# Causal score products in halves, new planner constants, and unread products early on TensorE

## The chip, the cores and the metric

The kernel runs as one program on one core of one Trainium2 chip. The metric is the device time of one execution in microseconds. Engines are named as in the profile: PE is TensorE's products, PEld its weight loads, DVE is VectorE, ACT is ScalarE, POOL is GpSimd, and SP issues the transfers from and to memory.

## The reference

A gated linear attention runs over 768 steps for 4 batches of 8 heads with 48 columns each; its output is the input of a layer of 8 experts, of which each token takes at most one. Cut to what matters:

```
a_re, a_im: scaled to a magnitude of at most 0.999
for t in range(S):                       # S = 768, per batch and head
    S_re, S_im = (a_re*S_re - a_im*S_im) + k[t] v[t]^T,  a_re*S_im + a_im*S_re
    y[t] = q[t] @ S_re
x = y as (3072 tokens, 384)
e = argmax(x @ w_gate); g = softmax(x @ w_gate)[e]; run only if x @ w_skip > 0
out = x + g * (relu(x @ w1[e]) @ w2[e])  # else out = x
```

## The kernel before

The recurrence is done in chunks of 128 steps: 6 chunks by 4 batches make 24 units, numbered u. For each unit the complex gate is turned into angles and decays ("gates": logarithms, exponentials and sines on ACT, sums over the steps as the triangular products `pt` and `pl` on PE). q and k are scaled and turned (`qe`, `w`, on DVE), transposed on PE (`tp`), and copied from PSUM (`wT`, on ACT). Inside a chunk the score of a key step and a query step matters only where the query is not earlier than the key. `pa` is the score product, four heads at a time: for each head a 96 by 128 weight (the keys) and 128 moving columns (the queries), all 128 by 128 scores, and `at` on DVE multiplies them by a triangular mask that zeroes the early queries. `py` makes the unit's output from the masked scores and the values `vt`, and from the state `Sb` that the chunks before have left. Its outputs are 64 wide, so that an even head writes PSUM partitions 0 to 63 and the odd head beside it 64 to 127. `ps` adds to the state, `yT` and `px` give the tokens and the routing scores.

After the last unit come the experts, eight after another: `ph` and `po` are their two products, and the gathered tokens `xg` come from memory, two buffers deep. Splitting the experts' weights into two parts on ACT and DVE (`h` and `l` in the trace) begins in the last units.

All operations of a unit are put into a list with an engine, a duration, a due time, what they need, and what buffers they take. `Plan.order` plays this list through: of the operations that can begin about as early as any, the one with the earliest due time is next on its engine. The instructions are then written in that order, and each engine works through its own in order. `STARTS`, `LEADS`, `TRIG`, `READY`, `PULL` and the other constants at the top set the due times; they say which units' gates go together and how early loads are asked for. SP issues all loads from one queue. fp32 products stand twice in the trace: each is two records, with a weight load each.

Of the kernel before, what the change touches and what calls it, by code (L numbers as in the profile page):

```python
# [10 lines left out]
F32 = mybir.dt.float32  # L11
F32R = mybir.dt.float32r
BF16 = mybir.dt.bfloat16
I32 = mybir.dt.int32
# [15 lines left out]
NEAR, COLD = 0.1, 33.0  # L30
WAFTER, WGAP, CHECK = 0.75, 0.21, 2
ROOMS = dict(ain=6, tr=5, U=6, cs=2, e=5, qk=4, w0=2, w1=2, wT0=2, wT1=2, vt=3, at=2, st=2, yT=2, row=4, G=1, raw=2, raw2=4,
             tp=2, pa=2, y=1, g=1, c=2, xa=3, mpt=2, mph=3, mpo=3, xg=2, xh=2, hh=2, og=2)
# [14 lines left out]
class Plan:  # L48
# [3 lines left out]
    OVER = dict(P=0.0, A=0.105, V=0.085, G=0.0)  # L52

    def __init__(self, rooms):
        self.rooms, self.ops, self.rel = rooms, {}, {}

    def add(self, key, eng, us, at, need=(), take=(), free=()):
        def put(fn):
            need_ = list(need)
            if (key[0], key[1] - 1) + key[2:] in self.ops and key[0][:2] not in ("rt", "ro", "re"):  # L60
                need_.append((None, (key[0], key[1] - 1) + key[2:]))
            self.ops[key] = (eng, us, at, need_, list(take), fn)
            for x in free:
                self.rel.setdefault(x, []).append(key)
        return put

    def order(self):
        end, free, held, out = {}, dict.fromkeys("PAVGS", 0.0), {"xa": [("xa", "z")]}, []
        pipe, warm = 0.0, [-9.0, 0.0]

# [31 lines left out]
        while todo:  # L102
            can = {}
            for key in todo:
                r, e = ready(key), self.ops[key][0][0]
                if r is not None:
                    can.setdefault(e, []).append((max(r, free[e]), self.ops[key][2], key))
            assert can, sorted(todo, key=str)[:9]
# [3 lines left out]
            todo.remove(key)  # L112
            eng, us, at, need, take, fn = self.ops[key]
            if len(eng) > 1:
                free[e] = max(s, pipe - 6.0) + (0.97 if e == "G" else 0.4 * int(eng[1]))
                pipe = max(free[e] + 0.9, pipe) + us
                end[key] = (free[e], "D", pipe + 1.0)
            else:
                if e == "P":
                    if s - warm[0] > 3.0:  # L120
                        warm[1] = 0.0
                    if s < COLD or warm[1] < 4.0:
# [12 lines left out]
        assert len(out) == len(self.ops), sorted((k for k in self.ops if k not in end), key=str)[:9]  # L135
        self.end = end
# [3 lines left out]
class Kern:  # L140
# [12 lines left out]
    def consts(self, ctx):  # L153
# [12 lines left out]
        for t, x in ((self.mask, 1.0), (self.turns, 0.5 / math.pi)):  # L166
            g.memset(t, x)
            sel(t, [[1, 128]], ALU.is_ge, 0.0, 0, -1)
        self.tri = cst.tile([128, 128], BF16, name="tri")
        g.memset(self.tri, 1.0)  # L170
# [78 lines left out]
    def gates(self, u, k, t, end):  # L249
# [59 lines left out]

        @add(("pt", u), "P", 0.75, t1, [("on" if c else "atan", u)], take=[("c", "pt", u)])  # L310
# [33 lines left out]

        @add(("pl", u), "P", 0.72, t2, [("U", u), ("pt", end - 1)], take=[("c", "pl", u)], free=[("U", u)])
# [43 lines left out]
    def ready(self, u, t):  # L389
# [15 lines left out]
        for k in range(2):  # L405
# [6 lines left out]
            for hh in range(2):  # L412
                @add(("tp", u, k, hh), "P", 0.455, t, [("w", u, k)], take=[("tp", u, k, hh)], free=[(f"w{k}", u)])
                def _(k=k, hh=hh):
# [18 lines left out]
    def unit(self, u):  # L433
# [6 lines left out]

        @add(("lv", u), "S1", 1.0, t - PULL, take=[("vt", u)])
        def _():
            vt = X["vt", u] = self.vts[u % len(self.vts)]
            nc.sync.dma_start(vt[:, :, 0:D], self.rows(self.v, c, b))

        for hh in range(2):
            @add(("pa", u, hh), "P", 0.91, t, [("wT", u, k, hh) for k in range(2)], take=[("pa", u, hh)], free=[("wT1", u)])
            def _(hh=hh):
                pa = X["pa", u, hh] = self.ps_at.tile([128, 4, C], F32, name=f"pa_{nm}_{hh}", tag="pa")
                for h in range(hh * 4, hh * 4 + 4):  # L450
                    PE.matmul(pa[:, h % 4], X["wT", u, 1][:, h], X["wT", u, 0][:, h], start=True, stop=True)  # L451

            @add(("at", u, hh), "V", 0.686, t, [("pa", u, hh)], take=[("at", u)], free=[("pa", u, hh)])
            def _(hh=hh):
                if ("at", u) not in X:
                    X["at", u] = self.un.tile([128, H, C], F32, name=f"at_{nm}", tag="at", bufs=self.rooms["at"])
                V.tensor_tensor(X["at", u][:, hh * 4:hh * 4 + 4], X["pa", u, hh],  # L457
                                self.mask.rearrange("p (o t) -> p o t", o=1).to_broadcast([128, 4, C]), ALU.mult)

# [6 lines left out]
        if not late:  # L466
            @add(("ps", u), "P", 1.41, t, [("w", u, 1), ("lv", u)], take=[("g", "ps", u)], free=[("w1", u), ("vt", u)])
            def _():
                ps = X["ps", u] = self.ps_g.tile([96, H, D], F32, name=f"ps_{nm}", tag="g")
                for h in range(H):  # L470
                    PE.matmul(ps[:, h], X["w", u, 1][:, h].rearrange("p k d -> p (k d)"), X["vt", u][:, h, 0:D], start=True, stop=True)

# [8 lines left out]
        for hh in range(2):  # L481
            @add(("py", u, hh), "P", 0.97 if c else 0.48, t,
                 [("at", u, hh), ("lv", u)] + ([("Sb", u), ("wT", u, 0, hh)] if c else []),
                 take=[("y", u)], free=[("at", u), ("vt", u), ("wT0", u)] + [("st", u)] * (c > 0))
            def _(hh=hh):
                if X.get("yof") != u:
                    X["yof"] = u
                    X["py"] = self.ps_y.tile([128, H // 2, C], F32, name=f"py_{nm}", tag="py")
                vt, at, qT, py = X["vt", u], X["at", u], X["wT", u, 0], X["py"]
                for hp in range(hh * 2, hh * 2 + 2):  # L490
                    for j in range(2):
                        PE.matmul(py[j * 64:j * 64 + 64, hp], vt[:, 2 * hp + j], at[:, 2 * hp + j], start=True, stop=(c == 0))  # L492
                    if c > 0:
# [9 lines left out]

        @add(("px", u), "P", 0.9, t, [("yT", u), ("wg", 0)], take=[bank], free=[("yT", u)])
        def _():
# [188 lines left out]
    def attention(self):  # L694
        with ExitStack() as ctx:
# [4 lines left out]
            self.ff, self.st, self.un = P("ff", 3), P("st", 2), P("un", 2)  # L700
            self.ps_tp, self.ps_at = P("ps_tp", 2, space=PSUM), P("ps_at", 2, space=PSUM)
# [3 lines left out]
            self.vts = [pers.tile([128, H, 64], F32, name=f"vt{i}") for i in range(self.rooms["vt"])]  # L705
            self.sts = [pers.tile([96, H, 64], F32, name=f"st{i}") for i in range(self.rooms["st"])]
            for t in self.vts + self.sts:
# [4 lines left out]
            self.pieces()  # L712
            self.order = self.plan.order()
# [103 lines left out]
    def experts(self):  # L817
# [26 lines left out]
        for e in range(E):  # L844
            te = T0 + TE * e

            @add(("xg", e), "S1", 1.1, te - 0.9, [("px", u)] + [(f"re{b}", 8) for b in range(B)], take=[("xg", e)])
            def _(e=e):
                xg = X["xg", e] = self.xp.tile([128, 2, XW], F32, name=f"xg_{e}", tag="xg")
                nc.sync.dma_start(xg, self.xs[e * CAP:(e + 1) * CAP].rearrange("(t p) d -> p t d", p=128))  # L850

            @add(("idx", e), "G", 0.2, te - 0.8, [("xg", e)])
            def _(e=e):
                X["idx", e] = self.xp.tile([128, 2], I32, name=f"idx_{e}", tag="idx")
                G.tensor_copy(X["idx", e], X["xg", e][:, :, DM])
# [18 lines left out]
            for j in range(NF):  # L874
                @add(("ph", e, j), "P", 1.08, te + j * 0.11,
                     [(x, e, t) for x in ("xh", "xl") for t in range(2)] + [("wl", e, k) for k in range(KD)] +
# [21 lines left out]
            for t in range(2):  # L898
                for j in range(NF):
                    @add(("po", e, t, j), "P", 0.52, te + 0.95 + (t * NF + j) * 0.053,  # L900
                         [("hl", e, j), ("wl", e, KD + j // 2)] + [(None, ("po", e, t, j - 1))] * (j > 0) + [("px", u)] * (e == 0),
# [250 lines left out]
```

## Time and profile before

| | us |
|---|---|
| median of 3 runs | 425.59 (425.2 to 426.17) |
| the profiled execution | 426.13 |
| its span, first to last instruction | 424.4 |
| PE busy in the span | 388.5 (92%) |
| DVE busy | 319.3 (75%) |
| ACT busy | 283.9 (67%) |
| PE products before the first `pt` (14.86 us into the span) | none |
| first and last start of `pa` | 33.4 and 256.8 |
| first and last start of `py` | 41.1 and 260.9 |

The attention's units fill the span to about 264 us, the experts the rest to about 412 us, and the last rows of the output and the end of the program follow. Busy times are averages over these stages: what a change is worth is read from the stage that it touches.

### The profile page before, as it was taken

The numbers are of one execution on the slowest core, as the hardware profiler recorded it, in microseconds if no ns is written. First come the engines' busy times: TensorE is split into PE (matmuls) and PEld (weight loads), VectorE is DVE, ScalarE is ACT, GpSimd is POOL, SyncE is SP. The second block draws the span as 40 slices with busy tenths as digits, with TensorE's granted clock in tenths as the row PEclk, the third lists the DMA queues.
The fourth block names the chain that finished last, engine by engine and source line by source line (L and its number), as shares of the span: only waits on it lengthen the run. The fifth ranks groups of instructions, "written<-read, shape, count | busy, mean of one in ns | idle before, by whom it ended". The sixth has DMA issues, their size and how long they took to land. (4 is left out here: it accounts for less than half of the span.)

```text
span 424.4 us, 8790 instructions
## 1 busy us (share of the span) xinstructions
PE 388.5 (92%) x3236; PEld 346.3 (82%) x3236; DVE 319.3 (75%) x722; ACT 283.9 (67%) x550; POOL 56.6 (13%) x94
## 2 busy tenths in 40 slices
PE   0569999999999999999999988899999999999992
PEld 0248689769868987997878977799999999999992
DVE  4469799979999978987997998877666676656220
ACT  5798998889798879849898654554454655446020
POOL 7000000014005003001300121101011010111101
PEclk9967999999999999999999999999999999999998
DMA  9999929986983892444423765586665766662001
GB/s 158 184 148 171 161 58 177 366 150 142 158 168 81 139 194 54 97 80 112 101 48 119 206 213 195 159 294 223 206 236 179 233 177 230 227 192 80 27 1 33
DMA packets 148049, 65.55 MB, mean 154 GB/s; under 512 B 129323, under 2 KB 143407, under 8 KB 148000
## 3 DMA queue, kind: packets, MB, share of 16 engines
q1 hardware_dynamic: 145440, 60.29, 60.7%
q0 software_dynamic: 2560, 4.63, 3.0%
q8 instruction: 28, 0.46, 0.5%
q14 instruction: 21, 0.17, 0.1%
HBM read 52.33 MB, written 15.77 MB: 160 GB/s over the span
## 5 line engine op out<-in xcount | busy, mean ns | idle before, releaser
L810 ACT CAST h<-r 128x768 fp32r<-128x768 f32 (+1 forms) x56 | 50.8, 926 | 38.5 <-issue 19.8
L815 DVE TENSOR_TENSOR l<-r,h 128x768 fp32r<-128x768 f32 (+1 forms) x56 | 58.9, 1069 | 7.8 <-ACT h L810 7.2
L558 POOL DMA_INDIRECT xs<-xa,sl x24 | 28.9, 1206 | 231.3 <-ACT tr L242 85.0
L418 PE MATMUL tp<-ident,w 128*96 128x128 f32 x384 | 55.0, 284 | 3.0 <-ACT wT L427 1.2
L886 PE MATMUL ph<-xh,h 128*128 128x256 f32 x192 | 54.6, 288 | 1.1 <-DVE hl L896 0.8
L418 PEld LDWEIGHTS tp<-ident,w 128*96 128x96 f32 x384 | 43.1, 131 | 14.6 <-issue 4.4
L427 ACT COPY wT<-tp 96x512 f32<-96x512 f32 x96 | 52.1, 580 | 2.8 <-PE tp L418 2.6
L886 PE MATMUL ph<-xh,l 128*128 128x256 f32 x192 | 53.6, 283 | 0.0
L451 PE MATMUL pa<-wT,wT 96*128 96x128 f32 x384 | 52.4, 284 | 0.1
L886 PE MATMUL ph<-xl,h 128*128 128x256 f32 x192 | 51.8, 283 | 0.3 <-DVE xl L872 0.3
L892 ACT ACTIVATE hh<-ph 128x256 fp32r<-128x256 f32 x64 | 24.3, 383 | 40.1 <-PE ph L886 40.1
L451 PEld LDWEIGHTS pa<-wT,wT 96*128 96x128 f32 x384 | 47.9, 197 | 2.3 <-issue 0.7
L410 DVE TENSOR_TENSOR w<-qk,cs 128x768 f32<-128x768 f32 x48 | 45.3, 951 | 0.2
L907 PE MATMUL po<-h,hh 128*128 128x384 f32 x128 | 43.6, 340 | 0.0
L896 DVE SCALAR_TENSOR_TENSOR hl<-ph,hh 128x256 fp32r<-128x256 f32 x64 | 26.2, 419 | 22.4 <-ACT hh L892 22.4
L909 PE MATMUL po<-h,hl 128*128 128x384 f32 x128 | 43.0, 336 | 0.0
L908 PE MATMUL po<-l,hh 128*128 128x384 f32 x128 | 43.0, 336 | 0.0
L492 PE MATMUL py<-at,vt 128*64 128x128 f32 x384 | 37.8, 282 | 1.6 <-DVE at L457 1.2
L886 PEld LDWEIGHTS ph<-xh,h 128*128 128x128 f32 x192 | 36.7, 191 | 2.2 <-DVE hl L896 1.0
L457 DVE TENSOR_TENSOR at<-pa,mask 128x512 f32<-128x512 f32 x48 | 32.6, 684 | 7.8 <-PE pa L451 7.7
L886 PEld LDWEIGHTS ph<-xh,l 128*128 128x128 f32 x192 | 36.6, 191 | 0.0
L313 PE MATMUL pt<-tr,turns 128*128 128x384 f32 x48 | 22.1, 563 | 15.3 <-ACT tr L242 14.9
(158 smaller groups left out, 774.1 us busy)
## 6 DMA issues: line engine op xcount, KB each, us to landing
r<-in_moe_w_dram SPq DMA_DIRECT2D x24, 512.0 KB, 4.7
r<-in_moe_w_dram SPq DMA_DIRECT2D x32, 384.0 KB, 4.0
ain<-in_a_re_dram SPq DMA_DIRECT2D x24, 192.0 KB, 4.3
ain<-in_a_im_dram SPq DMA_DIRECT2D x24, 192.0 KB, 4.5
qk<-in_q_dram SPq DMA_DIRECT2D x24, 192.0 KB, 3.9
qk<-in_k_dram SPq DMA_DIRECT2D x24, 192.0 KB, 4.2
vt<-in_v_dram SPq DMA_DIRECT2D x24, 192.0 KB, 3.3
out_dram<-xa SPq DMA_DIRECT2D x5, 768.0 KB, 5.2
```

Of the source, the lines that this page charges most:

```text
L410: V.tensor_tensor(n, X["qk", u][:, k].unsqueeze(2).to_broadcast([128, H, 2, D]), X["cs", c][:, b], ALU.mult)
L418: nc.tensor.transpose(tp[:, h], n[:, hh * 4 + h].rearrange("p k d -> p (k d)"), self.ident)
L427: (V.tensor_copy if onV else A.copy)(X["wT", u, k][:, hh * 4:hh * 4 + 4], X["tp", u, k, hh])
L451: PE.matmul(pa[:, h % 4], X["wT", u, 1][:, h], X["wT", u, 0][:, h], start=True, stop=True)
L457: V.tensor_tensor(X["at", u][:, hh * 4:hh * 4 + 4], X["pa", u, hh], self.mask.rearrange("p (o t) -> p o t", o=1).to_broadcast([128, 4, C]) ...
L492: PE.matmul(py[j * 64:j * 64 + 64, hp], vt[:, 2 * hp + j], at[:, 2 * hp + j], start=True, stop=(c == 0))
L810: nc.scalar.copy(X["W", e, n][0][:, ks], X["raw", e, i])
L815: nc.vector.tensor_tensor(lo[:, ks], X["raw", e, i], hi[:, ks], ALU.subtract)
L886: PE.matmul(ph, w[:, k, ks(j)], x[:, k], start=(i == 0), stop=(i == len(terms) - 1))
L907: PE.matmul(po, hh[:, j, ks(t)], w2h[:, j], start=(j == 0), stop=False)
L908: PE.matmul(po, hh[:, j, ks(t)], w2l[:, j], start=False, stop=False)
L909: PE.matmul(po, hl[:, j, ks(t)], w2h[:, j], start=False, stop=(j == NF - 1))
```

## The change

- **Score products in halves.** `pa` is eight products for four heads in place of four: for each head the 64 early keys against all 128 queries, and the 64 late keys against the 64 late queries alone. The part that causality empties is no longer computed. Each product writes 64 PSUM partitions, and the two halves of PSUM partitions get the same number of columns. An odd head has its early keys in the upper half, so its scores stand with the key steps exchanged; a second mask `masks[:, 1]` and a second copy of its values, `vs`, fit them. `vs` is loaded by two more transfers of 64 rows by four heads each from the same values. Two PSUM tiles `pas` are zeroed once on DVE, so the part that is never written is zero.
- **The plan.** New durations for `pa`, `py`, `tp` and others, a shift of the due time for 36 kinds of operation, other `STARTS`, `LEADS`, `PULL`, `READY`, `TRIG`, and 0.1 us on a PE operation that changes between the halved products (`py`, `pa`) and the rest. For the first two units two of the four `wT` copies go to DVE (`SHARE`). `xg` has three buffers and is asked for 1.69 in place of 0.9 units ahead (`FETCH`); the final check's due time moves by one expert (`CHECK`).
- **Unread products.** Where the plan sees PE idle, from 9 us of its own time up to the first `py`, it writes `n` products of `turns` by itself (128 by 128, fp32) into a PSUM tile that nobody reads, as many as fit at 0.23 us each with 0.25 us left over. It then counts PE as warm.

```diff
-STARTS = [0, 3, 7, 11, 15, 18, 21]
-AHEAD, TRIG, READY, PULL = 3.0, 0.63, 1.05, 3.44
+STARTS = [0, 3, 7, 11, 14, 18, 21]
+AHEAD, TRIG, READY, PULL = 3.0, 1.48, 1.28, 2.95
+FILL = 9.0
+SHIFT = {'rt4': 1.08, 'xl': 0.32, 'py': -0.87, ...}
-LEADS = {0: 5.96, 1: 3.48, 2: 2.07, 3: 1.5, 4: 2.5, 5: 2.37, 6: 2.26, 7: 2.47}
-SHARE = lambda u: ((0, 1), (1, 1)) if u < 0 else ()
+LEADS = {0: 7.67, 1: 3.67, 2: 2.09, 3: 2.19, 4: 3.21, 5: 1.9, 6: 1.57, 7: 2.34}
+SHARE = lambda u: ((0, 1), (1, 1)) if u < 2 else ()
...
+            n = int((s - max(free["P"], FILL) - 0.25) / 0.23)
+            if e == "P" and n > 0 and ("py", 0, 0) not in end:
+                out.append((max(free["P"], FILL), ("fill", len(out)), lambda n=n: self.fill(n)))
+                warm = [s, 9.0]
...
-        @add(("lv", u), "S1", 1.0, t - PULL, take=[("vt", u)])
+        @add(("lv", u), "S3", 1.6, t - PULL, take=[("vt", u)])
...
+            for lo, hi in ((slice(0, 64), slice(64, C)), (slice(64, C), slice(0, 64))):
+                nc.sync.dma_start(vs[hi, :, 0:D], v[lo, 1::2])
...
-            @add(("pa", u, hh), "P", 0.91, t, ...
+            @add(("pa", u, hh), "P", 0.62, t, ...
-                for h in range(hh * 4, hh * 4 + 4):
-                    PE.matmul(pa[:, h % 4], X["wT", u, 1][:, h], X["wT", u, 0][:, h], start=True, stop=True)
+                late, early, low, high = slice(64, C), slice(0, 64), slice(0, 64), slice(64, C)
+                for i, p, ts in ((1, high, early), (1, low, late), (0, high, late), (3, low, late),
+                                 (2, high, late), (0, low, early), (3, high, early), (2, low, early)):
+                    h = hh * 4 + i
+                    t0 = 0 if ts == early else 64
+                    PE.matmul(pa[p, i, t0:], k[:, h, ts], q[:, h, t0:], start=True, stop=True)
...
+    def idle(self, n):
+        if "warm" not in self.x:
+            self.x["warm"] = self.ps_y.tile([128, H // 2, C], F32, name="warm", tag="py")
+        for i in range(n):
+            self.nc.tensor.matmul(self.x["warm"][:, 0], self.turns, self.turns, start=True, stop=True)
```

The new masks are built by five more small operations on POOL among the constants.

## Rows read from the trace of the kernel before

**Rows 1.** Busy us of each engine by stretch (instructions in brackets), clock, DMA.
```profile
0.00:14.80 14.80, 0.00 (x0) 0.00 (x0) 6.93 (x15) 9.67 (x16) 8.08 (x41) 1.00 1.19 166
14.80:26.90 12.10, 8.63 (x13) 2.98 (x13) 4.90 (x9) 9.94 (x20) 0.00 (x0) 0.90 1.19 155
26.90:38.70 11.80, 11.55 (x56) 10.26 (x56) 11.70 (x26) 9.69 (x21) 0.00 (x0) 0.53 1.02 168
38.70:60.00 21.30, 21.05 (x163) 16.44 (x164) 16.73 (x31) 20.84 (x41) 0.00 (x0) 1.00 0.85 141
...
100.00:140.00 40.00, 38.88 (x364) 32.82 (x362) 38.55 (x92) 34.95 (x72) 6.13 (x6) 1.00 0.77 145
...
264.00:300.00 36.00, 33.77 (x258) 32.50 (x257) 25.85 (x69) 17.89 (x34) 4.26 (x6) 1.00 0.71 231
```

**Rows 2.** The same view for the attention's full stretch.
```profile
43.00:264.00 221.00, 214.43 (x2067) 183.21 (x2067) 197.77 (x490) 181.29 (x359) 29.35 (x27) 1.00 0.64 143
```

**Rows 3.** What PE waited for: total us, times, longest.
```profile
PE pt L313 <- ACT tr L242: 14.9, 1, 14.9
PE pl L348 <- ACT e L242: 3.0, 1, 3.0
PE pt L862 <- DMA xg<-xs: 1.7, 4, 0.6
```

**Rows 4.** Timeline of PE, 14 to 39 us: start, length, records merged.
```profile
14.86 4.58 PE L313 MATMUL pt<-tr,turns 128*128 128x384 f32 x6 [14.86 <-ACT tr L242]
...
26.90 1.94 PE L418 MATMUL tp<-ident,w 128*96 128x128 f32 x8 [0.34 <-DVE w L410]
...
33.45 3.78 PE L451 MATMUL pa<-wT,wT 96*128 96x128 f32 x16
```

**Rows 5.** Timeline of PE, 100 to 140 us: a lone score block.
```profile
113.66 1.06 PE L451 MATMUL pa<-wT,wT 96*128 96x128 f32 x8
114.56 1.48 PE L471 MATMUL ps<-vt,w 128*96 128x48 f32 x16
```

**Rows 6.** Timeline of PE at 154 us: angle sums at full clock.
```profile
154.24 1.46 PE L313 MATMUL pt<-tr,turns 128*128 128x384 f32 x4
```

**Rows 7.** Timeline of PE, 248 to 257 us: score and output blocks in turn.
```profile
251.47 1.06 PE L451 MATMUL pa<-wT,wT 96*128 96x128 f32 x8
252.46 0.44 PE L492 MATMUL py<-at,vt 128*64 128x128 f32 x4
252.72 0.39 PE L495 MATMUL py<-wT,st 96*64 96x128 f32 x4
252.95 0.39 PE L492 MATMUL py<-at,vt 128*64 128x128 f32 x4
253.17 0.39 PE L495 MATMUL py<-wT,st 96*64 96x128 f32 x4
253.49 1.16 PE L451 MATMUL pa<-wT,wT 96*128 96x128 f32 x8
254.48 0.17 PE L646 MATMUL pr<-oh,tri 128*128 128x8 bf16 x1
```

**Rows 8.** Timeline of 0.06 us at the head of one output block.
```profile
158.39 0.14 PEld L492 LDWEIGHTS py<-at,vt 128*64 128x64 f32 x2 [0.24 <-DVE at L457]
...
158.40 0.33 PE L492 MATMUL py<-at,vt 128*64 128x128 f32 x2
```

**Rows 9.** Instructions of the output tile: ns min/median/max, first and last start.
```profile
L492 PEld LDWEIGHTS py<-at,vt x384: 132/136/138, 41.1 to 260.6; 128*64 128x64 f32 x192
```

**Rows 10.** Groups by line: busy us, mean ns of one.
```profile
L427 ACT COPY wT<-tp 96x512 f32<-96x512 f32 x96 | 52.1, 580 | 2.8 <-PE tp L418 2.6
```

**Rows 11.** Timeline of SP and of ACT near the start.
```profile
11.87 1.00 SPq L444 DMA_DIRECT2D vt<-in_v_dram  x1
...
6.26 0.61 ACT L242 ACTIVATE tr<-ain,col 128x384 f32<-128x384 f32 x1 [1.33 <-POOL twice L159]
```

More of the change, by code (lines that the diff above doesn't have):

```diff
@@ L52 @@
     OVER = dict(P=0.0, A=0.105, V=0.085, G=0.0)
+    HALVES = ("py", "pa")
     def __init__(self, rooms):
@@ L61, in put @@
                 need_.append((None, (key[0], key[1] - 1) + key[2:]))
-            self.ops[key] = (eng, us, at, need_, list(take), fn)
+            self.ops[key] = (eng, us, at + SHIFT.get(key[0], 0.0), need_, list(take), fn)
             for x in free:
@@ L68, in order @@
         end, free, held, out = {}, dict.fromkeys("PAVGS", 0.0), {"xa": [("xa", "z")]}, []
-        pipe, warm = 0.0, [-9.0, 0.0]
+        pipe, warm, mode = 0.0, [-9.0, 0.0], False
         left, users, base, todo = {}, {}, {}, set()
@@ L106, in order @@
                 if r is not None:
-                    can.setdefault(e, []).append((max(r, free[e]), self.ops[key][2], key))
+                    can.setdefault(e, []).append((max(r, free[e]) + 0.1 * (e == "P" and mode != (key[0] in self.HALVES)), self.ops[key][2], key))
             assert can, sorted(todo, key=str)[:9]
@@ L119, in order @@
                 if e == "P":
+                    mode = key[0] in self.HALVES
                     if s - warm[0] > 3.0:
                         warm[1] = 0.0
-                    if s < COLD or warm[1] < 4.0:
+                    if s < FILL + 6.0 or warm[1] < 4.0:
                         us *= 2
@@ L134, in order @@
                     start(x)
-        assert len(out) == len(self.ops), sorted((k for k in self.ops if k not in end), key=str)[:9]
+        assert len(end) == len(self.ops), sorted((k for k in self.ops if k not in end), key=str)[:9]
         self.end = end
@@ L168, in consts @@
             sel(t, [[1, 128]], ALU.is_ge, 0.0, 0, -1)
+        self.masks = cst.tile([128, 2, 128], F32, name="masks")
+        g.tensor_copy(self.masks[:, 0], self.mask)
+        m = self.masks[:, 1]
+        g.memset(m[0:64, 0:64], 0.0)
+        g.memset(m[64:128, 64:128], 1.0)
+        g.tensor_copy(m[0:64, 64:128], self.mask[0:64, 0:64])
+        g.tensor_copy(m[64:128, 0:64], self.mask[64:128, 64:128])
         self.tri = cst.tile([128, 128], BF16, name="tri")
@@ L308, in _ @@
                 V.scalar_tensor_tensor(first, X["row", u - B], -2 * math.pi, first, ALU.mult, ALU.add)
-        @add(("pt", u), "P", 0.75, t1, [("on" if c else "atan", u)], take=[("c", "pt", u)])
+        @add(("pt", u), "P", 0.73, t1, [("on" if c else "atan", u)], take=[("c", "pt", u)])
         def _():
@@ L343, in _ @@
             self.table(X["cs", c][:, b, :, 0], X["tr", u][:, 0], AF.Sin, scale=-2 * math.pi, bias=self.hpi)
-        @add(("pl", u), "P", 0.72, t2, [("U", u), ("pt", end - 1)], take=[("c", "pl", u)], free=[("U", u)])
+        @add(("pl", u), "P", 0.73, t2, [("U", u), ("pt", end - 1)], take=[("c", "pl", u)], free=[("U", u)])
         def _():
@@ L412, in ready @@
             for hh in range(2):
-                @add(("tp", u, k, hh), "P", 0.455, t, [("w", u, k)], take=[("tp", u, k, hh)], free=[(f"w{k}", u)])
+                @add(("tp", u, k, hh), "P", 0.468, t, [("w", u, k)], take=[("tp", u, k, hh)], free=[(f"w{k}", u)])
                 def _(k=k, hh=hh):
@@ L439, in unit @@
         t = float(u)
-        @add(("lv", u), "S1", 1.0, t - PULL, take=[("vt", u)])
+        @add(("lv", u), "S3", 1.6, t - PULL, take=[("vt", u)])
         def _():
-            vt = X["vt", u] = self.vts[u % len(self.vts)]
-            nc.sync.dma_start(vt[:, :, 0:D], self.rows(self.v, c, b))
+            vt, vs = X["vt", u] = self.vts[u % len(self.vts)]
+            v = self.rows(self.v, c, b)
+            nc.sync.dma_start(vt[:, :, 0:D], v)
+            for lo, hi in ((slice(0, 64), slice(64, C)), (slice(64, C), slice(0, 64))):
+                nc.sync.dma_start(vs[hi, :, 0:D], v[lo, 1::2])
         for hh in range(2):
-            @add(("pa", u, hh), "P", 0.91, t, [("wT", u, k, hh) for k in range(2)], take=[("pa", u, hh)], free=[("wT1", u)])
+            @add(("pa", u, hh), "P", 0.62, t, [("wT", u, k, hh) for k in range(2)], take=[("pa", u, hh)], free=[("wT1", u)])
             def _(hh=hh):
-                pa = X["pa", u, hh] = self.ps_at.tile([128, 4, C], F32, name=f"pa_{nm}_{hh}", tag="pa")
-                for h in range(hh * 4, hh * 4 + 4):
-                    PE.matmul(pa[:, h % 4], X["wT", u, 1][:, h], X["wT", u, 0][:, h], start=True, stop=True)
+                pa = X["pa", u, hh] = self.pas[hh]
+                q, k = X["wT", u, 0], X["wT", u, 1]
+                late, early, low, high = slice(64, C), slice(0, 64), slice(0, 64), slice(64, C)
[4 more added lines that the diff above has]
+                    PE.matmul(pa[p, i, t0:], k[:, h, ts], q[:, h, t0:], start=True, stop=True)
             @add(("at", u, hh), "V", 0.686, t, [("pa", u, hh)], take=[("at", u)], free=[("pa", u, hh)])
@@ L456, in _ @@
                     X["at", u] = self.un.tile([128, H, C], F32, name=f"at_{nm}", tag="at", bufs=self.rooms["at"])
-                V.tensor_tensor(X["at", u][:, hh * 4:hh * 4 + 4], X["pa", u, hh],
-                                self.mask.rearrange("p (o t) -> p o t", o=1).to_broadcast([128, 4, C]), ALU.mult)
+                two = lambda x: x.rearrange("p (a j) t -> p a j t", j=2)
+                V.tensor_tensor(two(X["at", u][:, hh * 4:hh * 4 + 4]), two(X["pa", u, hh]),
+                                self.masks.unsqueeze(1).to_broadcast([128, 2, 2, C]), ALU.mult)
         if c > 0:
@@ L470, in _ @@
                 for h in range(H):
-                    PE.matmul(ps[:, h], X["w", u, 1][:, h].rearrange("p k d -> p (k d)"), X["vt", u][:, h, 0:D], start=True, stop=True)
+                    PE.matmul(ps[:, h], X["w", u, 1][:, h].rearrange("p k d -> p (k d)"), X["vt", u][0][:, h, 0:D], start=True, stop=True)
             @add(("T", u), "V", 0.55, t, [("ps", u)] + [("Sb", u)] * (c > 0), free=[("g", "ps", u)] + [("st", u)] * (c > 0))
@@ L481, in unit @@
         for hh in range(2):
-            @add(("py", u, hh), "P", 0.97 if c else 0.48, t,
+            @add(("py", u, hh), "P", 0.90 if c else 0.45, t,
                  [("at", u, hh), ("lv", u)] + ([("Sb", u), ("wT", u, 0, hh)] if c else []),
@@ L488, in _ @@
                     X["py"] = self.ps_y.tile([128, H // 2, C], F32, name=f"py_{nm}", tag="py")
-                vt, at, qT, py = X["vt", u], X["at", u], X["wT", u, 0], X["py"]
+                (vt, vs), at, qT, py = X["vt", u], X["at", u], X["wT", u, 0], X["py"]
                 for hp in range(hh * 2, hh * 2 + 2):
                     for j in range(2):
-                        PE.matmul(py[j * 64:j * 64 + 64, hp], vt[:, 2 * hp + j], at[:, 2 * hp + j], start=True, stop=(c == 0))
+                        PE.matmul(py[j * 64:j * 64 + 64, hp], vs[:, hp] if j else vt[:, 2 * hp], at[:, 2 * hp + j], start=True, stop=(c == 0))
                     if c > 0:
@@ L502, in unit @@
         bank = ("c" if late else "g", "px", u)
-        @add(("px", u), "P", 0.9, t, [("yT", u), ("wg", 0)], take=[bank], free=[("yT", u)])
+        @add(("px", u), "P", 0.925, t, [("yT", u), ("wg", 0)], take=[bank], free=[("yT", u)])
         def _():
@@ L704, in attention @@
             self.rooms = dict(ROOMS)
-            self.vts = [pers.tile([128, H, 64], F32, name=f"vt{i}") for i in range(self.rooms["vt"])]
+            self.vts = [[pers.tile([128, n, 64], F32, name=f"{a}{i}") for a, n in (("vt", H), ("vs", H // 2))] for i in range(self.rooms["vt"])]
+            self.pas = [self.ps_at.tile([128, 4, C], F32, name=f"pa{i}") for i in range(2)]
+            for x in self.pas:
+                nc.vector.memset(x, 0.0)
             self.sts = [pers.tile([96, H, 64], F32, name=f"st{i}") for i in range(self.rooms["st"])]
-            for t in self.vts + self.sts:
+            for t in [x for p in self.vts for x in p] + self.sts:
                 nc.gpsimd.memset(t[:, :, D:64], 0.0)
@@ L712, in attention @@
             self.pieces()
+            self.plan.fill = self.idle
             self.order = self.plan.order()
@@ L845, in experts @@
             te = T0 + TE * e
-            @add(("xg", e), "S1", 1.1, te - 0.9, [("px", u)] + [(f"re{b}", 8) for b in range(B)], take=[("xg", e)])
+            @add(("xg", e), "S1", 1.1, te - FETCH, [("px", u)] + [(f"re{b}", 8) for b in range(B)], take=[("xg", e)])
             def _(e=e):
-                xg = X["xg", e] = self.xp.tile([128, 2, XW], F32, name=f"xg_{e}", tag="xg")
+                xg = X["xg", e] = self.xp.tile([128, 2, XW], F32, name=f"xg_{e}", tag="xg", bufs=3)
                 nc.sync.dma_start(xg, self.xs[e * CAP:(e + 1) * CAP].rearrange("(t p) d -> p t d", p=128))
@@ L874, in experts @@
             for j in range(NF):
-                @add(("ph", e, j), "P", 1.08, te + j * 0.11,
+                @add(("ph", e, j), "P", 1.1, te + j * 0.11,
                      [(x, e, t) for x in ("xh", "xl") for t in range(2)] + [("wl", e, k) for k in range(KD)] +
@@ L899, in experts @@
                 for j in range(NF):
-                    @add(("po", e, t, j), "P", 0.52, te + 0.95 + (t * NF + j) * 0.053,
+                    @add(("po", e, t, j), "P", 0.526, te + 0.95 + (t * NF + j) * 0.053,
                          [("hl", e, j), ("wl", e, KD + j // 2)] + [(None, ("po", e, t, j - 1))] * (j > 0) + [("px", u)] * (e == 0),
```

12 lines of the change are left out of this document (7 added, 5 removed).

## The prediction

> **What bounds the kernel now.** I read the busy times by stretch first. From 43 to 264 us PE is busy 214.43 of 221 us, DVE 197.77, ACT 181.29 [rows 2]: in the attention PE sets the pace, and the others have 23 and 40 us to spare. The first 43 us are of another kind. PE does nothing for 14.8 us, and then waits for ACT's chain, which holds 9.94 of the next 12.1 us [rows 1]; the list of waits names it, 14.9 us once and 3.0 us later [rows 3]. From 26.9 to 38.7 us PE is full (11.55 of 11.8), but its granted clock averages 0.53, the lower of its two levels (1.2 GHz, where 1 is 2.4 GHz) for nearly all of it, and DVE is full beside it (11.70) [rows 1]. From 38.7 to 60 us ACT is full (20.84 of 21.3). In the experts PE is the bound again, 33.77 of 36 us [rows 1].
>
> So a us of PE time saved in the middle is worth up to a us, until DVE is full, and a us saved in the start is worth something only where ACT and DVE don't hold PE up anyway.
>
> **The score blocks.** One block (4 heads, 8 records) starts 0.90 us before what follows it on PE [rows 5]; its length of 1.06 is longer because the last records' ends overlap. That is 0.112 per record, and 48 blocks take 43 us.
>
> How fast halved products go, `py` shows, whose products already write 64 partitions: the two halves' weight loads start within 0.01 us of each other, two of 0.132 to 0.138 us in 0.14 [rows 8, 9], and so do the two products (0.33 us for both). Four records of 128 columns take 0.22 us [rows 7], so that two halves pass in the 0.11 us of one record. A new block has in each half 128 + 64 + 64 + 128 columns, 384, each in two records: 3 x 2 x 0.11 = 0.66 us, if the halves run by themselves and a product of 64 columns takes 0.055. No row shows one of 64 columns. Below, the bound is 0.66; above, 0.88, where each of the eight pairs takes 0.11 as with 128 columns. I take 0.66, since the halves in `py` start as if they didn't wait for each other. 0.90 - 0.66 = 0.24, by 48: -11.5 us; at the upper bound -1.
>
> In the written order the pairs are not equal (128 with 64, 64 with 64, 64 with 128, 128 with 128). If products start strictly in the order written, the upper half's later products wait for its neighbour's and the block takes 448 columns: 3.5 x 0.22 = 0.77 us, -6.2 us in all. In `py` all products have 128 columns, so these rows can't tell the two apart. The Trainium skill ("TensorE: Matmul & The Clock Gate", section "The mechanism") says that products start and end strictly in program order also when they lie on different parts of the array; by that the block would be the one of 448 columns. That case is a rival below.
>
> **What a change of mode costs.** From the last four records of `py` to a score block 0.32 us pass (253.17 to 253.49) in place of 0.22, and that block takes 0.99 in place of 0.90. From a score block to `py` 0.99 pass, and the first four records take 0.26 in place of 0.22 [rows 5, 7]. So leaving costs some 0.19 and entering 0.13, about 0.15 for an edge. Now that `pa` is of `py`'s mode, an edge between them goes, and one between `pa` and `tp`, `px` or `ps` comes. In the timeline from 43 to 262 us I count 34 entries into a score block from full-width work, 32 exits to it, and 13 contacts with `py` (such places are [rows 5, 7]). In the same order that is 66 edges more and 13 less: 53 x 0.15 = +8.0 us. With the plan's 0.1 us on an edge, all score blocks could stand beside `py`: 0. I take the middle, +4. Score and output: -7.5 us (from -11.5 to +7).
>
> **The start.** PE at full clock from the first unit on: the first six `pt` records took 4.58 us where four later took 1.46 [rows 4, 6]; a transposing block took 1.94 and two score blocks 3.78 us [rows 4], against 2 x 0.90 at full clock. The work from 26.9 to 38.7 us, 11.55 us at 0.53, would be 6.1: 5.4 us less for PE. It is worth that only where nothing else is full, and there DVE was full, and ACT behind it [rows 1]. Two `wT` copies for each of two units leave ACT, 4 x 0.58 = 2.3 us [rows 10]. Bounds 0 and 5.4 us and the 1 to 1.5 us by which the `pt` and `pl` chains get shorter; I take -3.
>
> The unread products cost nothing as long as PE would idle; they do it in order, though, and at the lower clock one takes 0.45 (four cold score records take 0.9 [rows 4]) where the plan counts 0.23. The first gap (9 to about 15 us of the plan) gets some 24: 5.5 us as planned, 10.8 cold. They need only `turns`, which POOL has long before, so they would begin near 3 us and end by 14. A later gap of the length of that behind `pl` (3.0 us [rows 3]) could be overrun by some 2.5 us if the clock were still low. I take 0.
>
> Also in the start: two more transfers per unit, 98 KB, on a queue that was issuing one after another at 1 us each [rows 11] with the DMA engines at 1.19 [rows 1]; at 166 GB/s 0.6 us a unit. Two units' worth stands ahead of the first output: 0 to 2 us, I take +0.8. Later the DMA share is 0.64 [rows 2], and loads are asked for units ahead: 0. Five more POOL operations, about 0.2 us each, stand among the constants, and ACT did wait 1.33 us for POOL at 6.26 us [rows 11]: 0 to 1.3, I take +0.6. Zeroing `pas` falls into DVE's idle time at the start.
>
> **The rest of the plan.** PE's idle time from 43 to 264 is 6.6 us [rows 2]. New due times could take half of it, or add as much: I take -1. Two copies of `wT` go to DVE only in the first two units: 2.8 us of DVE work at most, in the range of the start. The third `xg` buffer and the earlier request can take away the 1.7 us of waits for `xg` [rows 3]: -0.8. The check moves between gaps of DVE: 0.
>
> Sum: -7.5 - 3 + 0.8 + 0.6 - 1 - 0.8 = -10.9 us. Against the profiled execution's 426.13 (span 424.4, and 1.7 around it) that is 415.2. The median of the runs was 0.5 below it, so I predict 415.
>
> **The rivals.**
> *The halves keep the written order.* A block takes 0.77, the blocks save 6.2, less 4 for the edges, and the rest is as above (-3.4): -5.6, about 420. For it: nothing in `py` contradicts it. Against it: the two halves in `py` seem to go side by side.
> *DVE or ACT takes over.* In its fullest 40 us DVE reached 38.55 [rows 1]; at this share its 198 us fill 205, so that the middle can't be under 205 of 221 us. Short of this bound, ACT's full stretch (38.7 to 60) gives back what the warm start gained, and part of PE's savings turns into waits for `w` and `at`: half of 7.5 and none of the start, -4 to -6, about 420. The spare 23 us of DVE speak against it.
> *A better plan than I allow.* No new edges, all of the 5.4 us in the start, and half of PE's idle time gone: -11.5 - 5.4 - 3.3, and +0.6 net of the loads, POOL and `xg`: -19.6, about 406.
> *Loads show.* A load of 64 columns takes 0.136 us [rows 9] and hides behind a product of 128 columns. If a product of 64 columns can't hide it, each half pays 8 x 0.136 = 1.09 a block: +0.19 by 48 = +9, +4 for the edges, -3.4 for the rest: slower, about 435. It ends slower once a block takes over 0.90. Against it: in `py` the second pair's loads don't wait for the first ones' products.
> *No gain in the blocks.* At 0.88 a block, -1 + 4 - 3.4: 425, no change.
>
> **How the numbers follow.** Chances: the forecast (409 to 418) 0.48; the written order 0.16; DVE or ACT 0.12; the better plan 0.13; no gain 0.05; loads 0.06. 0.2% (0.9 us) is about what can be told from no change here. Faster: the first four, 0.89. The same: 0.04. Slower: loads and part of the no-gain case, 0.07. The range reaches from 405, the better plan, to 423, the written order with 3 us more of start costs; that leaves out the last two cases and the ends of the others, some 2 in 10.
>
> **What would show it.** A score block about 0.66 us from its start to that of an output block beside it; 0.77 or 0.88 would be the rivals. `pa` next to `py` in most places of PE's timeline, and fewer than 53 edges more. PE's busy time from 43 us to the last score shorter by 7 to 8 us, DVE's and ACT's the same in a shorter stretch, so DVE's share above 0.92. Granted clock 1 before 26 us and the first `tp` block near 1 us rather than 1.94; and the first score block earlier than 33.45 us by 2 to 4. The prediction is wrong if the stretch from the first score to the last (33.4 to 256.8) is not shorter, or if the start is later because unread products stand ahead of the first `pt`.

## The result and the profile after

The changed kernel takes 419.45 us (median of 4 runs, 418.12 to 420.88) against 425.74 of the kernel before: ratio 0.9854, interval 0.983 to 0.9878, 6.3 us faster. Forecast were 415 and a range of 405 to 423. The profiled execution is the fastest of the four, 418.12 us with a span of 416.4.

Busy us of each engine by stretch (instructions in brackets), then clock, DMA share and GB/s, of the changed kernel:

```profile
26.90:38.70 11.80, 10.31 (x103) 8.82 (x103) 11.73 (x25) 10.09 (x20) 0.00 (x0) 1.00 0.78 149
38.70:60.00 21.30, 20.66 (x206) 16.44 (x205) 20.99 (x41) 20.54 (x43) 0.00 (x0) 1.00 0.85 148
60.00:100.00 40.00, 38.37 (x461) 32.20 (x460) 39.29 (x94) 37.56 (x76) 2.06 (x1) 1.00 0.99 217
100.00:140.00 40.00, 38.26 (x480) 32.98 (x477) 37.83 (x90) 33.86 (x69) 11.07 (x10) 1.00 0.99 182
140.00:180.00 40.00, 38.49 (x459) 32.78 (x457) 35.54 (x84) 32.51 (x66) 9.25 (x5) 1.00 0.57 117
43.00:264.00 221.00, 208.13 (x2512) 178.81 (x2510) 200.93 (x516) 179.75 (x357) 35.15 (x28) 1.00 0.73 160
```

Against [rows 1] the granted clock from 26.9 to 38.7 us is 1.00 and not 0.53. Against [rows 2] PE is less busy (208.13, was 214.43) and DVE more (200.93, was 197.77). DVE is now full from 38.7 to 100 us: 20.99 of 21.3 (was 16.73 [rows 1]) and 39.29 of 40 (was 36.59, the third busy time here):

```profile
60.00:100.00 40.00, 39.12 (x372) 32.43 (x371) 36.59 (x88) 35.63 (x74) 5.77 (x5) 1.00 0.85 196
```

PE's timeline of the start, with the unread products (`warm`):

```profile
2.74 7.58 PE L752 MATMUL warm<-turns 128*128 128x128 f32 x44 [2.74 <-POOL turns L169]
14.97 2.93 PE L330 MATMUL pt<-tr,turns 128*128 128x384 f32 x4 [4.64 <-ACT tr L259]
...
28.00 1.08 PE L435 MATMUL tp<-ident,w 128*96 128x128 f32 x8 [0.57 <-DVE w L427]
...
32.00 0.93 PE L476 MATMUL pa<-wT,wT 96*64 96x128 f32 x16
```

The first gap's 22 products run from 2.74 to 10.3 us, PE idles for 4.6 us, and the first `pt` comes as late as before (14.97, was 14.86) and as slowly (4 records in 2.93 us). The granted clock, third from the end, says why:

```profile
10.30:14.97 4.67, 0.03 (x1) 0.00 (x1) 3.13 (x7) 3.69 (x6) 1.13 (x5) 0.96 1.46 187
14.97:17.70 2.73, 2.73 (x5) 1.52 (x6) 0.43 (x1) 1.26 (x3) 0.00 (x0) 0.50 1.43 186
18.90:21.10 2.20, 1.81 (x7) 1.17 (x7) 1.50 (x4) 2.20 (x6) 0.00 (x0) 1.00 1.43 186
```

At 7.8 us the unread products become faster (a record every 0.11 us, every 0.21 before). Then PE idles, and at 14.6 us the granted clock falls to 0.50, just ahead of the first `pt`. From 18.1 us it is 1.00 again and stays there through the attention; the unread products in the later gaps, up to 38.2 us, stand between the real ones. (Up to a trace's first clock record, at 7.8 us here and 21.0 in the kernel before, the 1.00 of such a row is no reading; that holds for the first row of [rows 1] and half of the second.) At the first transposing block PE is fast: 1.08 us, was 1.94 [rows 4]. The first score block starts 1.4 us earlier, the first output block 5.6 us later (46.7, was 41.1), because the plan puts the next units' gates ahead of it, on DVE too (the first `at` begins at 45.9 us, was 38.6).

The score blocks stand in pairs, 22 of the 23 pairs right behind an output block (PE's timeline of 60 to 100 us):

```profile
61.08 0.27 PE L518 MATMUL py<-at,vt 128*64 128x128 f32 x1
61.08 0.27 PE L518 MATMUL py<-at,vs 128*64 128x128 f32 x1
...
61.30 1.56 PE L476 MATMUL pa<-wT,wT 96*64 96x64 f32 x32
62.78 0.64 PE L435 MATMUL tp<-ident,w 128*96 128x128 f32 x4
```

Two blocks take 1.48 us from start to what follows, with the 0.10 by which the next start is late when the mode is left (0.32 in place of 0.22 [rows 7]): 0.69 for one, was 0.90 [rows 5]. The first records of this pair:

```profile
L476 PE MATMUL pa<-wT,wT x6: 219/222/274, 61.3 to 61.5; 96*64 96x64 f32 x4, 96*64 96x128 f32 x2
```

Four records of 64 columns, two products of the lower half, have started by 61.47 us beside two of 128, one product of the upper half. In the written order a product of 64 columns of the upper half stands between those two, and it has to let the one of 128 pass, whose second record starts at 61.42 us. So the halves don't wait for each other.

How much work each engine had before the first expert product, and how long it stood idle there (us; unread products count as PE work, 18 us):

| | first `ph` at | PE busy, idle | DVE busy, idle |
|---|---|---|---|
| before | 270.9 | 245.1, 25.7 | 230.2, 40.6 |
| after | 265.6 | 242.1, 23.5 | 231.2, 34.3 |

Without the unread products PE has some 21 us less to do, and the experts begin 5.3 us earlier. DVE has as much to do as before. The experts themselves (first to last `ph`) take 135.1 us, were 137.5; their last `po` starts at 408.9 us, was 416.6, so that they filled the span to about 417 us and not 412.

### The profile page after: what moved, and what is told of

Same layout as the page of the kernel before. It is cut to its first block, busy times and chain, and to the rows that moved or that the text cites. A ratio compares the mean times of both kernels' runs of the same rounds, so it can differ in the third digit from the quotient of the medians.

```text
span 416.4 us, 9865 instructions
## 1 busy us (share of the span) xinstructions
PE 384.8 (92%) x3742; PEld 346.6 (83%) x3742; DVE 320.3 (77%) x728; ACT 280.6 (67%) x546; POOL 65.5 (16%) x102
## 5 line engine op out<-in xcount | busy, mean ns | idle before, releaser
L584 POOL DMA_INDIRECT xs<-xa,sl x24 | 34.2, 1423 | 217.7 <-DVE lg L547 86.5
L435 PE MATMUL tp<-ident,w 128*96 128x128 f32 x384 | 52.2, 275 | 2.4 <-DVE w L427 1.7
L444 ACT COPY wT<-tp 96x512 f32<-96x512 f32 x92 | 50.4, 583 | 3.9 <-PE tp L435 3.6
L435 PEld LDWEIGHTS tp<-ident,w 128*96 128x96 f32 x384 | 41.4, 128 | 8.6 <-issue 3.7
L476 PE MATMUL pa<-wT,wT 96*64 96x128 f32 (+1 forms) x768 | 38.2, 249 | 0.8 <-DVE wT L444 0.5
L518 PE MATMUL py<-at,vt 128*64 128x128 f32 x192 | 36.2, 279 | 0.6 <-DVE at L483 0.5
L518 PE MATMUL py<-at,vs 128*64 128x128 f32 x192 | 36.1, 278 | 0.0
L923 PEld LDWEIGHTS ph<-xl,h 128*128 128x128 f32 x192 | 35.6, 191 | 0.0
L476 PEld LDWEIGHTS pa<-wT,wT 96*64 96x64 f32 x768 | 34.0, 137 | 1.8 <-issue 0.7
```

Of the source, the lines that this page charges most:

```text
L435: nc.tensor.transpose(tp[:, h], n[:, hh * 4 + h].rearrange("p k d -> p (k d)"), self.ident)
L444: (V.tensor_copy if onV else A.copy)(X["wT", u, k][:, hh * 4:hh * 4 + 4], X["tp", u, k, hh])
L476: PE.matmul(pa[p, i, t0:], k[:, h, ts], q[:, h, t0:], start=True, stop=True)
L518: PE.matmul(py[j * 64:j * 64 + 64, hp], vs[:, hp] if j else vt[:, 2 * hp], at[:, 2 * hp + j], start=True, stop=(c == 0))
L584: self.nc.gpsimd.indirect_dma_start(out=self.xsv[c * B + b], out_offset=bass.IndirectOffsetOnAxis(ap=sl, axis=0), in_=xa[:, b], in_offset= ...
L923: PE.matmul(ph, w[:, k, ks(j)], x[:, k], start=(i == 0), stop=(i == len(terms) - 1))
```

## The experiments

The kernel before ran beside each group of experiments again, with medians of 425.0 to 425.6 us. The ratios in brackets are to these, with their intervals. Differences from the changed kernel are of medians; taken from the ratios, some come out up to 1 us larger. Either way each is known to about 1.5 us only.

**The changed kernel without its unread products**

```diff
-        for i in range(n):
+        for i in range(0):
             self.nc.tensor.matmul(self.x["warm"][:, 0], self.turns, self.turns, ...)
```

> The changed kernel with its plan and order as they are, but none of the unread products is issued. Theory (the middle is now held by DVE, and PE has time to spare): PE is cold at its first tp, ps and pa blocks, 2 to 5 us late at the first score block, and 1 to 3 us of it are left at the end: about 421 to 422. Rival (PE still sets the pace, so that every us of the cold blocks shows): the 5.4 us of the prediction and the longer pt and pl, about 424 to 426. Second rival (the start is held by ACT and DVE alone): within 0.5 us of 419.5.

422.67 us (0.9945, 0.9923 to 0.9966): 3.2 us more (3.9 by the ratios), a little over the theory's range. Its PE timeline:

```profile
28.42 1.94 PE L435 MATMUL tp<-ident,w 128*96 128x128 f32 x8 [0.94 <-DVE w L427]
...
34.37 1.60 PE L476 MATMUL pa<-wT,wT 96*64 96x128 f32 x16 [0.67 <-ACT wT L444]
```

and its stretch from 26.9 to 38.7 us, with the granted clock third from the end:

```profile
26.90:38.70 11.80, 9.07 (x57) 7.19 (x58) 10.47 (x22) 8.77 (x18) 0.00 (x0) 0.50 0.81 154
```

The blocks are at the lower level again (0.50), the first score block is 2.4 us later and the first output block 3.2 us (49.9). About what is lost there is lost at the end.

**The changed kernel with full-width score blocks**

```diff
-                for i, p, ts in ((1, high, early), (1, low, late), ...):
-                    PE.matmul(pa[p, i, t0:], k[:, h, ts], q[:, h, t0:], start=True, stop=True)
+                for h in range(hh * 4, hh * 4 + 4):
+                    PE.matmul(pa[:, h % 4], k[:, h], q[:, h], start=True, stop=True)
```

> The changed kernel with its plan and order as they are, but the score blocks as before: four products of 128 columns and 128 outputs per block, one plain mask, one copy of the values, two transfers fewer per unit. A block goes from 0.69 to 0.90 us, 48 x 0.21 = 10 us of PE, and py and pa are of different modes again, so that about 25 edges between them come back at 0.15: +14 us of PE. Theory (DVE is full from 38 to 140 us, PE had idle time there): half of it or less shows, 424 to 427. Rival (PE sets the pace all along): 430 to 434.

421.1 us (0.9899, 0.9871 to 0.9926): 1.6 us more than the changed kernel (1.9 by the ratios), less than either theory. PE has 8.4 us more work before the experts (250.5) and 5.2 less idle time; two blocks take 1.89 us in place of 1.48. The edges expected to come back didn't: the trace has 52 changes of mode, the changed kernel's 58. So the halves do what they were made for, and most of it becomes idle time of PE. The 1.6 us are net of the two more transfers per unit that the halves need.

**The kernel before with the halves alone**

```diff
 # against the kernel before, whose constants, order and durations stay; with vs, masks and their loads
-                for h in range(hh * 4, hh * 4 + 4):
-                    PE.matmul(pa[:, h % 4], X["wT", u, 1][:, h], X["wT", u, 0][:, h], start=True, stop=True)
...
+                    PE.matmul(pa[p, i, t0:], k[:, h, ts], q[:, h, t0:], start=True, stop=True)
```

> The kernel before with the score products in halves, the second mask and the second copy of the values, and nothing else: its old plan, old durations and order, no unread products. Blocks save 48 x 0.21 = 10 us of PE; some 66 edges come and 13 go, +8 us at 0.15. Theory: a gain of 1 to 4 us only, 422 to 425, because the order puts score blocks between full-width work. Rival (edges are cheap, about 0.05): 417 to 420. Second rival (the edges cost more than the halves save): over 426.

428.13 us (1.0069, 1.0044 to 1.0093): slower, the second rival. Here the score blocks stand between full-width work:

```profile
112.48 0.88 PE L466 MATMUL pa<-wT,wT 96*64 96x64 f32 x16
113.33 1.14 PE L525 MATMUL px<-wg,yT 128*128 128x105 f32 x8
114.31 1.04 PE L425 MATMUL tp<-ident,w 128*96 128x128 f32 x8
115.28 0.93 PE L466 MATMUL pa<-wT,wT 96*64 96x128 f32 x16
```

Each lone block takes 0.85 to what follows in place of 0.90, and 132 changes of mode stand in the trace where the kernel before has 76. PE's work before the experts stays the same (244.4, was 245.1): 10 us saved, some 9 paid for 56 edges, 0.16 each. The extra 3 us are more than that. The two more transfers per unit and POOL's operations are in this kernel too, and part of the 3 us stands in the start: the first `pt` is 0.5 us later (15.34) and the first output block 1.2 us (42.30), and the granted clock is 0.50 until 41.3 us, where in the kernel before it was so until 38.0. The rest was not taken apart.

**Two xg buffers again**

```diff
-FETCH = 1.69
+FETCH = 0.9        # and xg=2, bufs=2
```

> The changed kernel with two xg buffers and the request 0.9 units ahead, as before. Theory: the waits of PE for xg come back, 0.8 to 1.7 us, 420.3 to 421.2. Rival (the experts are shorter for another reason): within 0.5 us of 419.5.

419.85 us (0.9862, 0.9833 to 0.9891): 0.4 us more, within the interval, the rival by its number. But in its trace the experts take 137.0 us and not 135.1, and PE waits 2.3 us for `xg`. In the five kernels here with two buffers PE waits 0.6 to 4.4 us for `xg` there, in those with three at most 0.4. What the third buffer gives (0 to 1.9) stays open.

**More work for DVE, in the kernel before and in the changed one**

```diff
             V.tensor_tensor(X["qk", u], X["qk", u], X["e", u], ALU.mult)
+            V.tensor_tensor(self.spare..., X["qk", u][:, 0], X["qk", u][:, 1], ALU.mult)
```

> The kernel before with one more DVE product of 128 x 384 per unit behind qe, whose result nobody reads: 24 x 0.55 = 13 us more of DVE, order unchanged. If PE sets the pace of the kernel before, 0 to 4 us slower (425 to 429), for DVE had 23 us to spare between 43 and 264 us; if DVE already shared the pace there, 5 to 9 us slower.

439.37 us (1.032, 1.029 to 1.035): 14.3 us more (13.6 by the ratio) for 13 us of work, in the kernel before, where DVE was idle for 23 of 221 us.

> The changed kernel with the same product more on DVE per unit, 13 us. Theory (after the change DVE sets the pace of the middle, and that is why the halves brought only 1.6 us): 8 to 13 us slower than the changed kernel, 427 to 432, and clearly more than the same product costs the kernel before. Rival (what holds the middle is the order and its chains from engine to engine, with no engine full): 3 to 7 us, like in the kernel before.

433.63 us (1.0198, 1.0168 to 1.0227): 14.2 us more for the same work, over both ranges, and not clearly more than in the kernel before, as the theory had it. So DVE is as decisive after the change as before it, and before it more than both expectations held possible. What DVE waited for from 100 to 220 us, first in the kernel before:

```profile
DVE at L457 <- PE pa L451: 2.2, 2, 1.9
DVE tr L322 <- ACT tr L317: 1.9, 3, 0.9
DVE se L601 <- ACT dl L242: 1.6, 1, 1.6
```

and with the additional work:

```profile
DVE at L458 <- PE pa L452: 2.2, 2, 1.9
DVE tr L322 <- ACT tr L317: 1.9, 3, 0.9
DVE se L602 <- ACT dl L242: 1.6, 1, 1.6
```

The same waits, of the same length, and up to the first `ph` DVE is idle for 39.7 us, was 40.6. (In the changed kernel a wait of 2.2 us for ACT's `e` goes and others come: 35.3 us of idle time, was 34.3.) So more work moves the waits and fills next to none of them: the idle 23 us from 43 to 264 us were no room. A reason that fits is that DVE waits there for chains that themselves began behind its earlier work; no run shows it by itself. The additional product stands on the chain from `qe` to `w`; that it would cost as much elsewhere was not tried. The products for PE below stand on the same chain, one step on, and cost less.

**More work for ACT**

```diff
             self.table(X["e", u][:, 1], X["pl", u], AF.Exp, scale=-0.5, ...)
+            A.copy(self.spare..., X["e", u][:, 0])
```

> The changed kernel with one more ACT copy of 128 x 384 per unit behind e1, read by nobody: 24 x 0.5 = 12 us more of ACT, order unchanged. DVE theory: 1 to 5 us slower (420 to 425), less than the product on DVE. If ACT sets the pace: 8 to 12 us slower. Chains without a full engine: about as much as on DVE.

425.39 us (1.0001, 0.9982 to 1.0021): 5.9 us more for 12 us of work, half of it. ACT is between.

**More work for PE, in both kernels**

```diff
+                    for i in range(2 * (k == 0 and hh == 0)):
+                        nc.tensor.matmul(tp[:, 0], self.turns[:, 0:96], self.turns, start=True, stop=True)
                     for h in range(4):
                         nc.tensor.transpose(tp[:, h], ...)
```

> The kernel before with two unread products of 128 columns more in front of each unit's first transposing block: 24 x 0.45 = 10.7 us more of PE, order unchanged. Theory (already before the change it is DVE with its waits for ACT that sets the pace, and PE has room): 1 to 5 us slower, 426 to 430. Rival (the prediction's: PE sets the pace before the change, and DVE does so only after it): 8 to 11 us slower, 433 to 436.

432.62 us (1.018, 1.015 to 1.021): 7.0 us more for 10.7 us of work, between the two expectations. In its trace the first `ph` comes 4.9 us later (275.8, was 270.9), and the experts take 140.4 us, were 137.5, though no product was added there. PE waits for `xg` longer [rows 3]:

```profile
PE pt L864 <- DMA xg<-xs: 4.4, 5, 1.4
```

Whether the added products cause that wait is open; in the attention, where they stand, less than half of them shows.

> The changed kernel with the same two products per unit, 10.7 us more of PE. Theory: 1 to 3 us slower, 420.5 to 422.5, as the full-width score blocks with their 8 us more of PE cost 1.6. Rival (the products stand on the chain from w to tp, where each us counts): 5 to 10 us slower.

421.02 us (0.9915, 0.9887 to 0.9942): 1.6 us more for the same 10.7 (2.6 by the ratios), in the theory's range; in the trace the first `ph` comes 0.9 us later (266.5). This is the pair that tells: before the change two thirds of an added PE us show (under a half if the attention alone is counted), after it a seventh to a quarter (a tenth). The stretch from 43 to 264 us, of the changed kernel with the additional products:

```profile
43.00:264.00 221.00, 214.47 (x2592) 188.58 (x2592) 200.95 (x512) 180.24 (x359) 34.28 (x28) 1.00 0.73 159
```

PE is as busy here (214.47) as in the kernel before (214.43 [rows 2]), where I read it as the bound, and yet the kernel is only 1.6 us slower than the changed one. So PE's busy time didn't tell the bound. The Trainium skill ("Trainium Kernel Development and Optimization", section "Performance Expectations") calls matmul busy time a bad metric for how close a kernel is to roofline, because matmuls are pipelined. How close this one is no run here shows; the two rows add that it is a bad metric for the bound as well. The weight loads (PEld) are busy for less than DVE in both rows, 183.21 and 188.58 us against 197.77 and 200.95, which fits what the additions say.

**The plan alone**

```diff
 # full-width score blocks as above, and
-        for i in range(n):
+        for i in range(0):
             self.nc.tensor.matmul(self.x["warm"][:, 0], self.turns, self.turns, ...)
```

> The changed kernel with its plan and order, but with full-width score blocks and without the unread products. If the parts add up (unread products 3.2, halves 1.6), 424.3, 1 us under the kernel before. Rival (the halves and the unread products help each other, so that the second one matters less without the first): 421 to 423.5. Second rival (the plan is worse by itself): 425.5 or more.

422.77 us (0.994, 0.9917 to 0.9963): 2.8 us under the kernel before, more than the sum of the parts leaves; the first rival. With the other three the four cases are:

| | full-width blocks | halves |
|---|---|---|
| no unread products | 422.8 | 422.7 |
| unread products | 421.1 | 419.45 |

The halves bring nothing while PE is cold in the start, and 1.6 us where it is warm; the unread products bring 1.7 and 3.2 (1.7 and 3.9 by the ratios). The ratios' intervals are about 1.1 us to each side, so that the plan's 2.8 and the unread products' gain with the halves are shown; the halves' 1.6, the 1.7, and the help of the one for the other are at the edge of the noise.

**Work taken from DVE**

```diff
-        @add(("on", u), "V", 0.554, ...
-            V.scalar_tensor_tensor(first, X["row", u - B], -2 * math.pi, first, ALU.mult, ALU.add)
+        @add(("on", u), "G", 1.0, ...
+            g.tensor_scalar(row, row, -2 * math.pi, None, ALU.mult)
+            g.tensor_tensor(first, first, row, ALU.add)
```

> The changed kernel with the carry of the angle (on, one row of 384, 0.54 us of DVE 20 times) on POOL as two operations, and the plan made anew with on at 1.0 us on POOL; 11 us of DVE go away. DVE theory: 3 to 8 us faster than the changed kernel, 411 to 416. Rival (chains): within 2 us of 419.5, or slower since the chain of a unit's gates gets longer.

445.3 us (1.0438, 1.0392 to 1.0485), the rival. The groups of the two operations on POOL (busy us, mean ns of one, idle time before):

```profile
L326 POOL TENSOR_SCALAR row<-row 1x384 f32<-1x384 f32 x20 | 30.5, 1523 | 25.7 <-DMA row<-tr 24.2
...
L327 POOL TENSOR_TENSOR tr<-tr,row 1x384 f32<-1x384 f32 x20 | 21.6, 1082 | 47.8 <-issue 35.3 <-ACT tr L259 10.9 <-POOL row L326 0.3
```

2.6 us in place of 0.54, on the chain of each unit's gates, and 11 us less of DVE didn't help.

```diff
-            @add(("Sb", u), "V", 0.554, ...        V.tensor_tensor(X["Sb", u]...
+            @add(("Sb", u), "G", 1.1, ...          nc.gpsimd.tensor_tensor(X["Sb", u]...
```

> The changed kernel with the scaled state Sb (96 x 384, 0.55 us of DVE 20 times, needed late in a unit) on POOL, and the plan made anew with it at 1.1 us on POOL. 11 us of DVE go away. Theory (a us of DVE costs a us): 4 to 10 us faster than the changed kernel, 409 to 415. Rival (POOL takes longer than planned or slows DVE down beside it, and T and py wait for it): 420 or more.

424.0 us (0.9966, 0.9943 to 0.9989), slower than the changed kernel, the rival. One `Sb` took 1.30 us on POOL, and DVE, with 2 us less to do before the experts than in the changed kernel (229.1, others had taken the place), was idle 43.2 us in place of 34.3:

```profile
L490 POOL TENSOR_TENSOR st<-T,Fall 96x384 f32<-96x384 f32 x20 | 26.0, 1303 | 150.4 <-DVE Fall L404 102.6 <-PE py L521 30.6 <-DVE T L503 17.2
```

The order was made anew for both (for `Sb` with 72 changes of mode, the changed kernel has 58), so these two kernels mix the work moved with another order, and don't tell what DVE's relief alone would bring. No version tried beats the changed kernel.

## Why the prediction was right, and where it was off

The direction and the range held, the size did not: 6.3 us and not 10.6. That the time lies in the range is in part luck: the largest term, 7.5 us for score and output blocks, brought 1.6 to 1.9, and the plan, set at 1.8 with `xg`, made up for some of it with 2.8. Point by point:

- *What bounds the kernel.* This is the step that failed: "in the attention PE sets the pace, and the others have 23 and 40 us to spare". In the kernel before, 10.7 us of PE cost 7.0 (4.9 in the attention), and 13 us of DVE cost 14.3. DVE, with its waits for ACT and PE, held the pace all along as far as these additions tell (the DVE product was tried in one place only), and PE stood behind it. So work taken from PE pays only until it is out of the way, and that is soon: after the change 10.7 us of PE cost 1.6.
- *The score blocks.* 0.66 us was forecast, 0.69 measured; the loads of 64 columns are hidden, and the products don't wait in the written order (two blocks would have taken 1.54 us and the edge, not 1.48). The first records of the pair at 61.30 us show the same. The Trainium skill ("TensorE: Matmul & The Clock Gate", "The mechanism") says that products start and end strictly in program order, which would have given the 1.54. The trace disagrees, for products on two halves of the output partitions. The saving of work was as forecast, its worth (some 10 us at 1 us each) was not: 1.6 us.
- *The edges.* The price held: 0.16 in the old order, forecast 0.15, and 56 more of them, forecast 53. Their number in the new order didn't: 4 us were set for some 27 more, and there are 18 fewer (58, were 76).
- *The start.* -3 was forecast for PE at full clock; the unread products bring 1.7 (full-width blocks) or 3.2 (halves). That those of the first gap would begin near 3 us and stand in nobody's way is in the timeline. That the clock they raised would fall again before the first `pt` (14.6 us) was not foreseen, and the first score block came 1.4 us earlier, not 2 to 4.
- *Loads and POOL's constants.* +1.4 together was not tested by itself. In the old order (`halves_only`) the first output block is 1.2 us later. In the changed kernel ACT's wait for POOL at 6.26 us [rows 11] is gone, and the first `pt` is 0.1 us later, which leaves little of the 0.6.
- *The rest of the plan.* -1.8 with `xg`; the plan with the third buffer brings 2.8. DVE's idle time shows where: from 38.7 to 60 us DVE was busy for 16.73 us [rows 1], with the plan alone for 19.79, and is now for 20.99. In what order of due times this lies was not taken apart.

Of the rivals, the second (DVE takes over, part of PE's savings becomes waits, about 420) describes what came, with the correction that DVE didn't take over: it was there before. My argument against it, DVE's spare 23 us, was the wrong reading of [rows 2]. Of the signs, the stretch from the first score block to the last is shorter (216.7 us, was 223.4), as forecast, but DVE's share in it is 0.917 (was 0.894) and not above 0.92.

## What to carry to other kernels

Idle time of an engine is room only if its waits get shorter when it is given more to do. Here a us added to DVE, busy for 89% of the attention, cost a whole one, and 10.7 us added to PE at 94% (208.13 of 221 us, after the change) cost some 2. An unread operation per unit on each engine tells which, before any work is saved; put it in more than one place, and read in the trace in which stage the time is lost. Entering and leaving the halved mode (0.3 us) costs more than halving one score block saves (0.2), so that the order has to put blocks of one mode side by side first. Unread products on an idle TensorE cost nothing where they ended before the first real product, but PE idled behind them and the clock was at 0.50 again when that product began. With those in the later gaps, between the real products, the first units ran at full clock; the two kinds were not tried apart.

## What the runs showed of the hardware

Products on the two halves of the output partitions run side by side without waiting for their order, also where one has 64 columns and the other 128, with the weight loads hidden: 0.69 us a block where 0.66 is the sum of the columns. The granted clock was 0.50 from 14.6 to 18.1 us, after PE had stood idle from 10.3 us, and the first `pt` fell into it. A POOL operation on a single partition of 384 elements took 1.08 to 1.52 us, one on 96 partitions 1.30, where DVE takes 0.54 to 0.55 for either.
